# Top-32 attention and two MLPs on one core: PReLU with the threshold as bias, one reciprocal per pair, Mish in batches, and eight weight pieces split a round later

## The chip, the cores and the metric

The kernel runs on one core of one Trainium2 chip. Its time is the device time of one execution in microseconds (us); lower is better. The engines are PE (TensorE), DVE (VectorE), ACT (ScalarE), POOL (GpSimd) and SP, which here only issues DMAs.

## What is computed

Inputs are q, k, v of shape (2, 8, 576, 64) and four weight matrices in 64-bit floats. Cut to what matters:

```python
scores = scale * q @ k.T                                # 576 x 576 for each of 16 heads
kth = np.partition(scores, -32, axis=-1)[..., -32:-31]
scores = np.where(scores >= kth, scores, -1e9)          # 32 largest of each row stay
attn = np.exp(scores - max); attn = attn / (attn.sum() + 1e-9)
x = (attn @ v), heads side by side                      # 1152 tokens x 512
h = x @ w_in;  g = h * tanh(softplus(h));  x = g @ w_out     # MLP 1, Mish, d_ff = 2048
h = x @ w_in2; r = max(h, 0); out = (r * r) @ w_out2         # MLP 2, squared ReLU
```

## The kernel before

**Rounds, pairs, tiles.** The 1152 tokens go through in four rounds of 192, 320, 320 and 320. Attention for one round and two heads is a pair (20 pairs: 4, 4, 8, 4 by round, since round 2 takes 64 tokens of batch 0 and 256 of batch 1). A pair has one to five tiles of 128 rows, 72 in all: 12, 20, 20 and 20 by round. A tile (`tile_of`, L397) is: scores on PE (`ps`, L419), copied by ACT to `s`; the 32 largest of each row on DVE by four MAX8 and three MATCH_REPLACE8 (L435 to L439); two small POOL instructions that make biases from the 32nd value (L450, L451); a PReLU on ACT that pushes the smaller scores far down, then Exp with the row sum kept in `acc`; five PE transposes (L464, L466) and a copy to `pt`. `unit_end` (L486) inverts the sums of each unit of one or two tiles and spreads them (L492 to L499). `pair_end` (L503) multiplies by v (`px`, L519), transposes the inverses, and scales on DVE into `x` (L547).

**Weights.** The weights lie as 64-bit floats in 32 pieces of 1 MB. `convert` (L635 to L675) makes 32-bit floats: a PReLU on ACT, a TENSOR_SCALAR on POOL (L654), a SCALAR_TENSOR_TENSOR on DVE (L656, "combine" below). Round 0 multiplies by these in one float32 term. Meanwhile each piece is split into a high part (ACT, or POOL for every third) and a low part (four POOL subtractions of 256 columns, L294), and both parts are written back to DRAM. Rounds 1 to 3 fetch them (L700, 1 MB each) and use three fp32r products instead of one: `product`, L723.

**MLP.** Per round PE runs four phases of 64 output tiles by 128 rows: in (MLP 1), out, in (MLP 2), out. After the first, ACT applies Mish straight from PSUM and POOL subtracts for the low part `gl` (L283); after the third, ACT does ReLU, Square and the high part, POOL the low part. Mish and Exp lie in different ACT tables, so going from one to the other loads a table (ACT_TABLE_LOAD). Before a round, `x` is split into `xh` (ACT) and `xl` (DVE, L283).

**What sets the order.** The program is written by a small planner (`Order`, L82): each step is a generator that asks for an engine with a cost and a rank, and the instructions are emitted in the order in which the planner grants them. Each engine runs its own list strictly in that order, SP its list of DMA issues too. Buffers are counted by semaphores (`BUFS`): three `vt`, two `kr`, two `qr`, and seven 1 MB weight buffers (`ROLES`), which become the ring of fetched pieces when the conversion is done. `load(p)` takes kr, qr and vt together and starts when pair p-2 is prepared.

Of the kernel before, what the change touches and what calls it, by code (L numbers as in the profile page):

```python
# [18 lines left out]
UP = 2.0 ** 40  # L19
LOW3 = 2.0 ** -29 * (1.0 - 2.0 ** -12)  # L20
# [172 lines left out]
def topk_attention_two_mlps(  # L193
# [5 lines left out]
    v_rest: bass.AP,  # L199
# [106 lines left out]
    started, fast_done = Ev(), Ev()  # L306
    loaded, prepared = [Ev() for _ in pairs], [Ev() for _ in pairs]
# [6 lines left out]
    def load(p):  # L314
        b, s0, n = group(p)
        hp = pairs[p][2]
        h = slice(2 * hp, 2 * hp + 2)
        moves = []
        eng = nc.scalar if p == 0 else nc.sync
        halves = [slice(i * D, i * D + D) for i in range(2)]  # L320
        if owner[b, hp][0] == p:
            yield sems["kr"]
            kr = krs[p] = new([P, 2, S], F32, "kr")
            moves += [(kr[z], k[b, h].rearrange("h d s -> d h s"), 288) for z in halves]
        yield sems["qr"]
        qr = qrs[p] = new([P, 2, NMAX], F32, "qr")
        moves += [(qr[z, :, 0:n], q[b, h, :, s0:s0 + n].rearrange("h d s -> d h s"), n / 2) for z in halves]
        if p == 0:
            moves = [moves[i] for i in (0, 2, 1, 3)]
        yield sems["vt"]  # L330
        vt = vts[p] = new([P, 2, NK + 1, D], F32, "vt")
        last = [(vt[:, :, 0:NK, :], v[b, hp], 256), (vt[SR:P, :, NK, :], v_rest[b, hp], 32)]
        for i, (o, x, kb) in enumerate(moves):
            f = lambda o=o, x=x, e=eng if i % 2 else nc.sync: e.dma_start(out=o, in_=x)
            if i < len(moves) - 1:
                yield ("SP", 0.6, 5, f)
                sim.dma_free = max(sim.dma_free, sim.now + 0.8) + kb / 360.0
                if p == 0 and i == 1:
                    yield sim.dma_free - sim.now + 1.2
                    sim.set(started)  # L340
            else:
                yield from sim.dma(f, kb, 5)
        sim.set(loaded[p])
        for o, x, kb in last:
            yield ("SP", 0.6, 6, lambda o=o, x=x: nc.sync.dma_start(out=o, in_=x))
            sim.dma_free = max(sim.dma_free, sim.now + 0.8) + kb / 360.0

    def loads():
        for p in range(len(pairs)):
            if p > 1:  # L350
                yield prepared[p - 2]
# [45 lines left out]
    def tile_of(p, j, a, rank, unit, pair):  # L397
# [29 lines left out]
        yield act(0.65, 9, s.rearrange("p (a b) -> p a b", a=2), sp[:, :, 0:HK])  # L427
# [4 lines left out]
        nm = sb.tile([P, 2], F32, tag="nm", bufs=6, name="nm")  # L432
# [53 lines left out]
    def unit_end(j, unit, pair):  # L486

        acc, _, done = unit[:3]
        yield sems["r"]
        r_ = new([P, 2, D], F32, "r")  # L490
        z = acc if j < 2 else acc[:, 0:1]
        yield ("POOL", 0.35, 1, lambda: nc.gpsimd.tensor_scalar(out=z, in0=z, scalar1=1e-9, scalar2=None, op0=ALU.add))  # L492
        yield SLACK
        yield ("DVE", 0.16, 3, lambda: nc.vector.reciprocal(z, z))
        if j < 2:
            sums = acc[:, 0:2].rearrange("p (a o) -> p a o", o=1).to_broadcast([P, 2, D])
            yield ("POOL", 0.45, 1, lambda: nc.gpsimd.tensor_tensor(out=r_, in0=sums, in1=one2, op=ALU.mult))
        else:
            yield act(0.3, 10, r_, same, scale=z)  # L499
        pair["r"][j] = r_.rearrange("p a d -> p (a d)")  # L500
        sim.set(unit[5])

    def pair_end(p, units, pair):  # L503
# [3 lines left out]
        vt = vts[p]  # L507
        for u in units:
            for d in u[2]:
                yield d  # L510
        yield sems["ps_x"]
# [17 lines left out]
        for u in units:  # L529
            yield u[5]  # L530
        yield sems["ps_t"]
        pp = psum("t")

        def transposes():
            for t in range(nt):
                nc.tensor.matmul(pp[:, t * P:(t + 1) * P], pair["r"][t], ident, start=True, stop=True)
            if m:
                nc.tensor.matmul(pp[:, nt * P:n], pair["r"][2], sel, start=True, stop=True)

        yield ("PE", 0.25 * (nt + m), 7, transposes)  # L540
        for _ in range(nt + m):
            give("r")
        inv = sb.tile([P, NMAX], F32, tag="inv", bufs=1, name="inv")
# [7 lines left out]
        yield SLACK / 2
        yield ("DVE", 0.6, 4, scaled)
        give("ps_x")
        x1_left[r] -= 1
        if x1_left[r] == 0:
            sim.set(x1_done[r])

    def masks_done(j, unit, pair):
        for d in unit[1]:
            yield d  # L560
        yield from unit_end(j, unit, pair)

    x1_left = [HP * len(g) for g in ROUNDS]
# [68 lines left out]
    boths = Places(sim, [("w", i) for i in range(nw) if ROLES[i] == "b"], NP, to_ring)  # L632
    halves = Places(sim, [("half", i, h) for i in range(nw) if ROLES[i] == "w" for h in range(2)], NP - len(once), to_ring)

    def convert(i, raw_at):  # L635
# [26 lines left out]
        if HI[i % len(HI)] == "a":  # L662
# [271 lines left out]
```

## Time and profile before

| what | us |
|---|---|
| median of 3 runs | 714.75 |
| lowest, highest | 711.21, 715.51 |
| the profiled execution | 715.83 |
| its span, first to last instruction | 714.0 |

The span is what the trace shows; 1.8 us lie around it. All times of rows are counted from the span's start. PE is busy 608.3 us, DVE 447.2, ACT 435.6 and POOL 376.2. A busy time is a mean over stages with different limits, so the rows below are read stage by stage.

### The profile page before, as it was taken

To read this page: it belongs to the slowest core of one execution; us is meant where nothing else is said; L and a number is where in the kernel's file an instruction comes from. 1 tells how busy PE (TensorE), PEld (TensorE's weight loads), DVE (VectorE), ACT (ScalarE), POOL (GpSimd) and SP (SyncE) were. 2 spreads that over 40 slices of the span, in tenths; PEclk is the share of its full clock that TensorE was granted. 3 is DMA by queue.
4 is the path that set the end of the run, shared out by engine and by line. 5 is a ranking of instruction groups with operands and counts; after the bars stand their busy time and mean duration, and the time that the engine had idled before them with its cause. 6 is when DMAs were issued, how large, how long until landed. Compare 5 with 4: busy or idle time off the path is not lost.

```text
span 714.0 us, 11305 instructions
## 1 busy us (share of the span) xinstructions
PE 608.3 (85%) x4016; PEld 562.5 (79%) x4016; DVE 447.2 (63%) x841; ACT 435.6 (61%) x810; POOL 376.2 (53%) x584
## 2 busy tenths in 40 slices
PE   4344657789798778998889999989999999999997
PEld 2233447668796658898779999878899999999997
DVE  5978999888788884369788999999950000000000
ACT  3654767988488757854368955899745704512720
POOL 5998892489989997364455621334112401400410
PEclk9666779899999999999999999999999999999999
DMA  8786963377899899999966667643476888888850
GB/s 278 256 264 224 314 233 132 137 259 289 338 403 352 315 326 336 351 321 309 305 235 222 212 225 258 215 177 127 177 280 224 298 318 282 298 304 304 297 205 29
DMA packets 42362, 186.21 MB, mean 261 GB/s; under 512 B 8513, under 2 KB 19777, under 8 KB 21825
## 3 DMA queue, kind: packets, MB, share of 16 engines
q1 hardware_dynamic: 42016, 185.29, 74.1%
q8 instruction: 32, 0.52, 0.3%
q10 hardware_dynamic: 288, 0.20, 0.1%
q14 instruction: 26, 0.20, 0.1%
HBM read 149.55 MB, written 35.91 MB: 260 GB/s over the span
## 4 chain that ended last, share of the span: by engine, by line
PE 46%; POOL 26%; DMA 12%; ACT 7%; issue 4%; DVE 3%; SPq 0%; POOLq 0%; ACTq 0%; DVEq 0%
PE pm L723 39%; POOL w L294 10%; DMA qr<-in_q 5%; POOL stage L654 4%; DMA vt<-in_v 4%; DMA w<-both 3%; PE ps L419 2%; PE px L519 2%; ACT e L277 2%; ACT L277 2%; PE pt L464 2%; POOL w L287 2%; POOL w L654 2%; POOL kT L362 1%; POOL acc L492 1%
## 5 line engine op out<-in xcount | busy, mean ns | idle before, releaser
L723 PE MATMUL pm<-xh,w 128*128 128x320 f32 (+1 forms) x896 | 199.5, 315 | 3.9 <-DMA w<-both 1.8
L723 PE MATMUL pm<-gh,w 128*128 128x320 f32 x768 | 176.8, 312 | 0.0
L439 DVE MAX8 mx<-w 128x8 f32<-128x576 f32 x216 | 164.4, 761 | 7.4
L723 PEld LDWEIGHTS pm<-xh,w 128*128 128x128 f32 x896 | 152.3, 190 | 5.9 <-ACT h L277 2.2
L283 POOL TENSOR_TENSOR gl<-h,gh 128x320 fp32r<-128x320 f32 x96 | 83.5, 880 | 133.6 <-ACT gh L277 129.9
L723 PEld LDWEIGHTS pm<-gh,w 128*128 128x128 f32 x768 | 130.4, 189 | 0.4 <-issue 0.4
L723 PE MATMUL pm<-xl,w 128*128 128x320 f32 x384 | 119.7, 312 | 0.1
L723 PE MATMUL pm<-gl,w 128*128 128x320 f32 x384 | 119.1, 310 | 0.0
L438 DVE MATCH_REPLACE8 w<-mx,w 128x576 f32<-128x576 f32 x144 | 107.0, 743 | 0.0
L464 PE MATMUL pt<-ident,e 128*128 128x128 f32 x288 | 50.3, 303 | 56.0 <-ACT e L277 45.6
L277 ACT ACTIVATE e<-s,nm 128x576 f32<-128x576 f32 x72 | 55.5, 773 | 60.5 <-POOL nm L450 60.3
L294 POOL TENSOR_TENSOR w<-w,w 128x256 fp32r<-128x256 f32 x112 | 84.0, 779 | 9.1 <-ACT w L277 7.9
L464 PEld LDWEIGHTS pt<-ident,e 128*128 128x128 f32 x288 | 37.1, 153 | 64.4 <-ACT e L277 51.0
L723 PEld LDWEIGHTS pm<-xl,w 128*128 128x128 f32 x384 | 73.0, 190 | 0.3 <-DVE xl L283 0.3
L277 ACT ACTIVATE pt<-pt 128x640 f32<-128x640 f32 x72 | 50.8, 705 | 36.2 <-PE pt L466 35.8
L723 PEld LDWEIGHTS pm<-gl,w 128*128 128x128 f32 x384 | 72.6, 189 | 0.0
L277 ACT ACTIVATE h<-pm 128x320 f32<-128x320 f32 (+1 forms) x112 | 45.8, 422 | 37.9 <-PE pm L723 30.5
L435 DVE MAX8 mx<-s 128x8 f32<-128x576 f32 x72 | 53.7, 745 | 22.7 <-ACT s L277 22.7
L277 ACT ACTIVATE e<-e,nm 128x576 f32<-128x576 f32 x72 | 55.9, 776 | 6.0
L277 ACT ACTIVATE s<-ps 128x576 f32<-128x576 f32 x72 | 45.9, 637 | 12.7 <-PE ps L419 12.7
L438 DVE MATCH_REPLACE8 w<-mx,s 128x576 f32<-128x576 f32 x72 | 53.5, 743 | 0.0
L519 PE MATMUL px<-pt,vt 128*64 128x320 f32 (+7 forms) x400 | 50.6, 393 | 2.1 <-ACT pt L277 1.9
(101 smaller groups left out, 938.1 us busy)
## 6 DMA issues: line engine op xcount, KB each, us to landing
w<-both SPq DMA_DIRECT2D x96, 1024.0 KB, 5.0
both<-w SPq DMA_DIRECT2D x32, 1024.0 KB, 5.4
stage<-in_weights SPq DMA_DIRECT2D x22, 1024.0 KB, 6.1
w<-in_weights SPq DMA_DIRECT2D x10, 1024.0 KB, 5.9
vt<-in_v SPq DMA_DIRECT2D x20, 256.0 KB, 8.6
kr<-in_k SPq DMA_DIRECT2D x16, 288.0 KB, 12.6
qr<-in_q SPq DMA_DIRECT2D x16, 160.0 KB, 5.4
out_x<-y SPq DMA_DIRECT2D x8, 160.0 KB, 3.5
```

Of the source, the lines that this page charges most:

```text
L277: op = ("ACT", t, rank, lambda: nc.scalar.activation(out, in_, func, **kw))
L283: return ({"g": "POOL", "v": "DVE"}[e], t, rank, lambda: eng.tensor_tensor(out=out, in0=in0, in1=in1, op=ALU.subtract))
L287: return ("POOL", 0.08 + 0.00113 * n, rank, lambda: nc.gpsimd.tensor_copy(out=out, in_=in_))
L294: yield ("POOL", 0.05 + 0.0024 * n, rank, lambda: nc.gpsimd.tensor_tensor(out=out[:, z], in0=in0[:, z], in1=in1[:, z], op=op))
L419: nc.tensor.matmul(sp[:, i, 0:HK], q_, k_[:, i * HK:(i + 1) * HK], start=l == 0, stop=l == len(steps) - 1)
L435: nc.vector.max(out=mx[:, 0, :], in_=s)
L438: nc.vector.match_replace(out=w, in_to_replace=mx[:, i - 1, :], in_values=s if i == 1 else w, imm_value=LOWEST)
L439: nc.vector.max(out=mx[:, i, :], in_=w)
L464: nc.tensor.transpose(pp[:, c * P:(c + 1) * P], e[:, c * P:(c + 1) * P], ident)
L519: nc.tensor.matmul(xo[a * D:(a + 1) * D, 0:n], vt[z, a, c, :], pt[z, a, c, 0:n], start=c == 0, stop=c == NK)
L654: yield ("POOL", 1.3, 4, lambda: nc.gpsimd.tensor_scalar(out=lo, in0=lo.bitcast(U32), scalar1=LOW3, scalar2=-0.499, op0=ALU.mult, op1=ALU. ...
L723: nc.tensor.matmul(o, w[a], x[b], start=first and i == 0, stop=last and i == len(terms) - 1)
```

## The change

- **PReLU's bias is the threshold.** The copy of the scores multiplies by 2^40, PReLU computes threshold minus score with the 32nd value as bias, and Exp turns the sign back. One POOL instruction per tile goes (L450), and PReLU no longer waits for POOL; Exp still needs `nm`.
- **Sums inverted per pair.** One add on POOL and one reciprocal on DVE for all sums of a pair; PE spreads them by multiplying the broadcast sums with the identity (`spread`), beside the last tiles and not after px. `r`, `sel` and `same` go.
- **Mish in batches** (`BATCHES`: 4, 4, 4, 2, 2 tiles in rounds 0 to 2): ACT copies each tile to an SBUF buffer `hs` and runs Mish, then the high part, over a batch.
- **Squares** move from ACT to POOL in rounds 0 to 2 and to DVE in round 3 (`RELU`).
- **x split early**: each 128-row chunk of x is split when its pairs are done (`prepare_x`), not when all are.
- **Late pieces**: pieces 24 to 31 are not split in round 0 (`AHEAD`); they are kept as 512 KB of float32, fetched in round 1 into a second buffer, split there, and written back for rounds 2 and 3. All high parts are ACT's now (`HI`).
- **Loads**: v has its own process (`load_v`), so k and q no longer wait for a `vt` buffer. k, q and v are laid out on the host so that each is one DMA. `ROLES` has six buffers instead of seven; `hs` takes two of 4 x 320 columns.

```diff
-BUFS = {"s": 3, "e": 2, "r": 3, "w": 2, "kr": 2, "vt": 3, "qr": 2, "kT": 4, "h": 3, "x1": 2, "pt": 1, "y": 2}
+BUFS = {"s": 3, "e": 2, "w": 2, "kr": 2, "vt": 3, "qr": 2, "kT": 4, "h": 3, "hs": 2, "x1": 2, "pt": 1, "y": 2}
-HI = "aag"
-ROLES = "wwwbbbr"
+BATCHES = [[4, 4, 4, 2, 2]] * 3 + [[]]
+RELU = "pppv"
+XL = " vvv"
+HI = "a"
+AHEAD = 24
+ROLES = "wwwbbr"
...
+    def load_v():
+        for p in range(len(pairs)):
+            b = group(p)[0]
+            yield sems["vt"]
+            yield loaded[p]
+            vt = vts[p] = new([P, 2, NK + 1, D], F32, "vt")
+            yield from sim.dma(lambda: nc.sync.dma_start(out=vt, in_=v[b, pairs[p][2]]), 320, 6)
+            sim.set(v_loaded[p])
...
-        yield ("POOL", 0.7, 1, biases)
-
-        yield act(0.8, 8, e, s, AF.Prelu, "exp", bias=nm[:, 0:1], scale=UP, alpha=2.0 ** 120)
+        yield ("POOL", 0.38, 1, lambda: nc.gpsimd.tensor_scalar(out=nm, in0=thr, scalar1=mx[:, 0, 0:1], scalar2=scale / UP, op0=ALU.subtract, op1=ALU.mult))
+
+        yield act(0.8, 8, e, s, AF.Prelu, "exp", bias=thr, scale=-1.0, alpha=FALL)
         give("s")
-        yield act(0.85, 8, e, e, AF.Exp, "exp", bias=nm[:, 1:2], scale=scale / UP, accum_out=acc[:, a:a + 1])
+        yield act(0.98, 8, e, e, AF.Exp, "exp", bias=nm, scale=-scale / UP / FALL, accum_out=acc[:, a:a + 1])
...
+        def spread():
             for t in range(nt):
...
+                for a in range(2):
+                    nc.tensor.matmul(pp[a * D:(a + 1) * D, t * P:(t + 1) * P], acc[:, t, a:a + 1].to_broadcast([P, D]), ident, start=True, stop=True)
...
+        if i >= AHEAD:
+            kept[i] = dr.tile([P, n], F32, tag=f"k{i}", name=f"kept{i}")
+            sim.spawn(put_back(i, w_at))
+            yield from sim.dma(lambda: nc.sync.dma_start(out=kept[i], in_=w), 512, 15)
+            sim.set(kept_done[i])
+            return
...
+    def fetch_late(i, j, at, w_at):
+        rings[i] = at
+        both = shared[at].rearrange("p (a m) -> p a m", a=2)
+        ready[i] = [both[:, 0], both[:, 1]]
+        w = shared[w_at][:, 0:NW].bitcast(F32)
+        yield from sim.dma(lambda: nc.sync.dma_start(out=w, in_=kept[j]), 512, 12)
+        yield from split_w(j, both, w, HI1[j % len(HI1)], 7)
+        ring.append(w_at)
+        sim.give(ring_sem)
+        sim.set(got[i])
+        yield from store(j, both)
...
+        def batch(i0, m_, hs):
...
+                yield act(t, 2, hs[:, 0:m_, 0:n], hs[:, 0:m_, 0:n], AF.Mish, "mish")
+                yield act(t, 11, g[0][:, z, 0:n], hs[:, 0:m_, 0:n])
+                for i in range(0, m_, 2):
...
+                    yield sub("g", 2 * n, 5, g[1][:, u, 0:n], hs[:, y, 0:n], g[0][:, u, 0:n].bitcast(F32))
...
+            if RELU[r] == "p":
+                yield ("POOL", 0.1 + 0.0024 * n, 5, lambda: nc.gpsimd.tensor_tensor(out=h_out, in0=h, in1=h, op=ALU.mult))
+            elif RELU[r] == "v":
+                yield ("DVE", 0.2 + 0.001 * n, 3, lambda: nc.vector.tensor_tensor(out=h_out, in0=h, in1=h, op=ALU.mult))
```

Three places in the engines' lists follow. On DVE, where round 1's last x (`x_1141`, after the change `x_1189`) is scaled and split; `x_2212` and `x_2178` belong to round 2. Before:

```order
L439 MAX mx<-w 128x8
L547 TENSOR_TENSOR x_1141<-px,inv 128x320
L656 SCALAR_TENSOR_TENSOR w_93<-w_93,stage 128x1024
L438 MATCH_REPLACE w<-mx,w 128x576
L439 MAX mx<-w 128x8
L494 RECIPROCAL acc<-acc 128x1
L283 TENSOR_TENSOR xl<-x_1141,xh 128x320 x2
L547 TENSOR_TENSOR x_2212<-px,inv 128x64
L283 TENSOR_TENSOR xl<-x_1141,xh 128x320 x2
L435 MAX mx<-s 128x8
```

The same place after the change:

```order
L431 MAX mx<-w 128x8
L527 RECIPROCAL acc<-acc 128x1
L512 TENSOR_TENSOR x_1189<-px,inv 128x320
L427 MAX mx<-s 128x8
L430 MATCH_REPLACE w<-mx,s 128x576
L431 MAX mx<-w 128x8
L512 TENSOR_TENSOR x_2178<-px,inv 128x64
L430 MATCH_REPLACE w<-mx,w 128x576
L431 MAX mx<-w 128x8
L276 TENSOR_TENSOR xl<-x_1189,xh 128x320
```

All 32 combines and three of the four splits now stand ahead of the last x, which comes after tile 34 as before; only one split is left behind it.

On SP, the loads of k and q for the first pair of batch 1 (the first 576-column k of round 2) and the fetches of round 1 (`w<-both`) around them. Before:

```order
L345 DMA vt<-in_v_rest 64x2x64
L334 DMA kr<-in_k 64x2x576 x2
L334 DMA qr<-in_q 64x2x256 x2
L700 DMA w_2148<-both_704 128x2048
L700 DMA w_95<-both_789 128x2048
L700 DMA w_2216<-both_817 128x2048
L700 DMA w_96<-both_834 128x2048
L700 DMA w_2346<-both_1149 128x2048
L700 DMA w_2092<-both_1157 128x2048
L345 DMA vt<-in_v 128x2x256
L345 DMA vt<-in_v_rest 64x2x64
L334 DMA kr<-in_k 64x2x576 x2
```

After, from the first such load on:

```order
L321 DMA kr<-in_k 128x1152
L321 DMA qr<-in_q 128x2x256
L702 DMA w_1928<-both_367 128x2048
L645 DMA kept_1929<-w_85 128x1024
L645 DMA kept_1957<-w_86 128x1024
L961 DMA out_x<-y 128x192
L702 DMA w_1990<-both_370 128x2048
L702 DMA w_2002<-both_476 128x2048
L665 DMA both_2001<-w_88 128x2048
L702 DMA w_87<-both_518 128x2048
L645 DMA kept_2034<-w_86 128x1024
L321 DMA kr<-in_k 128x1152
```

The first of these loads now stands ahead of every fetch of round 1, the second behind four; before they stood behind six and twelve.

On POOL, in round 1's third phase (ReLU of MLP 2). Before:

```order
L283 TENSOR_TENSOR gl<-h,gh 128x320 x2
L450 TENSOR_SCALAR nm<-mx 128x1
L451 TENSOR_SCALAR nm<-mx 128x1
L492 TENSOR_SCALAR acc<-acc 128x2
L283 TENSOR_TENSOR gl<-h,gh 128x320 x2
```

After:

```order
L936 TENSOR_TENSOR h<-h 128x320 x2
L276 TENSOR_TENSOR gl<-h,gh 128x320
L441 TENSOR_SCALAR nm<-mx 128x1
L276 TENSOR_TENSOR gl<-h,gh 128x320
L287 TENSOR_TENSOR w_1928<-w_1990,w_1928 128x256 x3
L936 TENSOR_TENSOR h<-h 128x320
L276 TENSOR_TENSOR gl<-h,gh 128x320
```

The squares (L936) and the low parts of the first late piece (`w_1928<-w_1990`) stand between the subtractions that the next phase needs.

## Rows read from the trace of the kernel before

**Rows 1.** The page: busy tenths in 40 slices of 17.85 us

```profile
PE   4344657789798778998889999989999999999997
...
DVE  5978999888788884369788999999950000000000
...
POOL 5998892489989997364455621334112401400410
```

**Rows 2.** Stretches: us, then busy us (x count) by engine, granted clock, DMA share, GB/s

```profile
226.00:275.00 49.00, 36.21 (x254) 30.75 (x252) 38.48 (x69) 32.05 (x56) 45.26 (x64) 1.00 0.90 314
275.00:313.00 38.00, 35.45 (x268) 33.99 (x268) 15.10 (x33) 27.25 (x54) 23.46 (x32) 1.00 1.02 372
...
597.00:714.00 117.00, 113.08 (x768) 112.58 (x768) 3.54 (x8) 42.26 (x92) 28.07 (x32) 1.00 0.68 241
```

**Rows 3.** Groups by line, DVE, 8 to 265 us: busy, mean ns, idle before

```profile
L656 DVE SCALAR_TENSOR_TENSOR w<-w,stage 128x1024 int32<-128x1024 int32 x19 | 24.0, 1261 | 17.7 <-POOL stage L654 13.4 <-ACT w L277 4.2
L656 DVE SCALAR_TENSOR_TENSOR w<-w,w 128x1024 int32<-128x1024 int32 x9 | 11.5, 1275 | 6.5 <-POOL w L654 6.5
```

**Rows 4.** Timeline, DVE and PE, end of round 1's attention: start, us, instruction, idle

```profile
118.47 0.74 DVE L435 MAX8 mx<-s 128x8 f32<-128x576 f32 x1
...
124.08 0.74 DVE L435 MAX8 mx<-s 128x8 f32<-128x576 f32 x1
...
265.34 0.76 DVE L439 MAX8 mx<-w 128x8 f32<-128x576 f32 x1
...
271.44 0.99 DVE L283 TENSOR_TENSOR xl<-x,xh 128x320 fp32r<-128x320 f32 x2 [5.27 <-ACT xh L277]
...
274.81 0.41 PE L723 MATMUL pm<-xh,w 128*128 128x320 f32 x1
```

**Rows 5.** Groups by line, POOL, 113 to 275 us

```profile
L294 POOL TENSOR_TENSOR w<-w,w 128x256 fp32r<-128x256 f32 x84 | 64.3, 794 | 6.7 <-ACT w L277 5.6
...
L287 POOL CAST w<-w 128x1024 fp32r<-128x1024 f32 x7 | 10.4, 1488 | 0.3
...
L450 POOL TENSOR_SCALAR nm<-mx 128x1 f32<-128x1 f32 x20 | 6.5, 323 | 7.3 <-DVE mx L439 5.9
```

**Rows 6.** Timeline, ACT, one change from Mish to Exp in round 0

```profile
123.38 0.33 ACT L277 ACTIVATE first<-pm 128x192 f32<-128x192 f32 x1 [0.62 <-PE pm L723]
123.73 1.28 ACT L277 ACT_TABLE_LOAD   x1
125.03 0.78 ACT L277 ACTIVATE e<-s,nm 128x576 f32<-128x576 f32 x1
```

**Rows 7.** Timeline, SP's issues and the DVE tile that waited for them

```profile
281.86 1.46 SPq L334 DMA_DIRECT2D kr<-in_k  x2
285.22 4.30 SPq L334 DMA_DIRECT2D qr<-in_q  x2
291.42 8.65 SPq L700 DMA_DIRECT2D w<-both  x6
...
309.23 0.76 DVE L435 MAX8 mx<-s 128x8 f32<-128x576 f32 x1 [7.39 <-ACT s L277]
```

**Rows 8.** Waits of PE, 275 to 541 us: us in total, times, longest

```profile
PE pt L536 <- POOL r L497: 3.4, 1, 3.4
PE ps L419 <- POOL kT L362: 2.7, 2, 2.0
PE pt L464 <- ACT e L277: 2.6, 1, 2.6
```

**Rows 9.** Groups by line, whole run: high parts on ACT, transposes of inverses on PE

```profile
L277 ACT ACTIVATE w<-w 128x1024 fp32r<-128x1024 f32 (+1 forms) x28 | 30.4, 1086 | 2.3 <-DMA both<-w 1.7 <-DVE w L656 0.6
...
L536 PE MATMUL pt<-ident,r 128*128 128x128 f32 x56 | 10.0, 292 | 4.6 <-POOL r L497 3.4 <-ACT pt L277 1.2
```

**Rows 10.** Groups by line, POOL, 540 to 597 us, when DVE is idle

```profile
L283 POOL TENSOR_TENSOR gl<-h,gh 128x320 fp32r<-128x320 f32 x16 | 14.1, 879 | 25.6 <-ACT gh L277 24.7 <-PE pm L723 0.9
```

**Rows 11.** The page: DMA issues, KB each, us to landing

```profile
w<-both SPq DMA_DIRECT2D x96, 1024.0 KB, 5.0
```

More of the change, by code (lines that the diff above doesn't have):

```diff
@@ L484, in tile_of @@
         sim.set(done[a])
[L486 to L501, printed above, removed]
     def pair_end(p, units, pair):
@@ L506, in pair_end @@
         nt, m = tiles(n)
-        vt = vts[p]
+        for u in units:
+            for d in u[1]:
+                yield d
+        z = pair["acc"].rearrange("p u a -> p (u a)")[:, 0:2 * nt + m]
+        yield ("POOL", 0.33, 1, lambda: nc.gpsimd.tensor_scalar(out=z, in0=z, scalar1=1e-9, scalar2=None, op0=ALU.add))
+        sim.spawn(inverse(p, pair, z))
         for u in units:
@@ L510, in pair_end @@
                 yield d
+        yield v_loaded[p]
+        vt = vts[p]
         yield sems["ps_x"]
@@ L528, in pair_end @@
                 yield 0.5
[L529 to L543, printed above, removed]
+        yield pair["inv_done"]
+        inv = pair["inv"]
         o = sum(x[2] for x in ROUNDS[r][:gi])
@@ L547, in scaled, with inverse @@
             nc.vector.tensor_tensor(out=x1[r][:, hp, o:o + n], in0=xo[:, 0:n], in1=inv[:, 0:n], op=ALU.mult)
+        yield ("DVE", 0.25 + 0.0009 * n, 4, scaled)
+        give("ps_x")
+        x1_left[r][hp] -= 1
+        if x1_left[r][hp] == 0:
+            sim.set(x1_part[r][hp])
+        if not any(x1_left[r]):
+            sim.set(x1_done[r])
+    def inverse(p, pair, z):
+        n = group(p)[2]
+        nt, m = tiles(n)
+        acc = pair["acc"]
+        yield SLACK / 2
+        yield ("DVE", 0.16, 3, lambda: nc.vector.reciprocal(z, z))
+        yield sems["ps_t"]
+        pp = psum("t")
+        def spread():
+            for t in range(nt):
+                for a in range(2):
+                    nc.tensor.matmul(pp[a * D:(a + 1) * D, t * P:(t + 1) * P], acc[:, t, a:a + 1].to_broadcast([P, D]), ident, start=True, stop=True)
+            for a in range(2 * m):
+                h = slice(a * D, (a + 1) * D)
+                nc.tensor.matmul(pp[h, nt * P:n], acc[h, nt, 0:1].to_broadcast([D, D]), ident[h, h], start=True, stop=True)
+        yield ("PE", 0.25 * nt + 0.15 * m, 7, spread)
+        inv = pair["inv"] = sb.tile([P, NMAX], F32, tag="inv", bufs=1, name="inv")
         yield act(evict_time(n), 9, inv[:, 0:n], pp[:, 0:n])
         give("ps_t")
[L551 to L563, printed above, removed]
+        sim.set(pair["inv_done"])
+    x1_left = [[len(g)] * HP for g in ROUNDS]
+    x1_part = [[Ev() for _ in range(HP)] for _ in ROUNDS]
     def attention():
@@ L712, in release, with late @@
     def release(i):
+        def late():
+            yield both_done[i % NP]
+            ring.append(rings.pop(i))
+            sim.give(ring_sem)
         if i < NP:
@@ L715, in release @@
         else:
-            ring.append(rings.pop(i))
-            sim.give(ring_sem)
+            sim.spawn(late())
     def product(o, w, x, first, last):
@@ L892, in all_mlps @@
             yield from mlps(r)
-    for process in (loads(), preparations(), attention(), conversions(), fetches(), all_mlps()):
+    for process in (loads(), load_v(), preparations(), attention(), conversions(), fetches(), all_mlps()):
         sim.spawn(process)
```

217 lines of the change are left out of this document (128 added, 89 removed).

## The prediction

> **What bounds the kernel now.** I read the slices first [rows 1]. There the reader sees two halves. Up to about slice 16 (285 us) DVE and POOL stand at 8 or 9 tenths while PE stands at 4 to 8; from slice 21 on PE stands at 9 almost throughout, and in the last ten slices DVE has nothing to do. So the end is set by PE's work from the moment that it is fed, and that moment, the start of round 1, is set by DVE and POOL. The stretches [rows 2] put numbers to it: between 226 and 275 us POOL is busy 45.26 of 49 us (92%) and PE 36.21; in round 3, 597 to 714 us, PE is busy 113.08 us for 768 matmuls, 0.147 us each, at the full granted clock. A microsecond by which round 1 starts earlier is then a microsecond at the end, as long as PE is not starved later.
>
> Next, what holds up DVE before round 1. Back to back, a tile takes 124.08 - 118.47 = 5.61 us [rows 4]. Up to the end of tile 34, whose last MAX8 ends at 265.34 + 0.76 = 266.1 us [rows 4], DVE's list holds 34 tiles (191 us) and 32 combines of 1.26 us (40 us) [rows 3]: 231 us, plus the start-up and waits. The waits stand on the combines: 17.7 + 6.5 = 24.2 us, nearly 20 of them for POOL's TENSOR_SCALAR on the same piece [rows 3]. POOL is late because it is full: the low parts of pieces cost 84 x 794 ns in 113 to 275 us, the high parts that POOL makes 1488 ns each [rows 5].
>
> Last, the seam. Round 1's first matmul runs at 274.81, 8.7 us after tile 34's end; 5.27 of them are DVE's wait for `xh` before it can make `xl` [rows 4].
>
> **The change part by part.** The sum is made against the profiled execution, 715.8 us (span 714.0 and 1.8 around it), 1.1 above the median.
>
> *POOL before round 1.* By the lists, the stretch of tiles 13 to 32 loses 20 of 79 low-part instructions (20 x 0.794 = 15.9 us), six high parts (6 x 1.488 = 8.9) and one of two `nm` instructions in 20 tiles (20 x 0.323 = 6.5) [rows 5]; it gains 16 squares of 192 columns, by columns 0.879 x 192 / 320 = 0.53 us each [rows 10], 8.4 us. Net 23 us less on an engine that was 92% busy at the end of that stretch [rows 2], so the TENSOR_SCALAR that a combine waits for stands in a shorter queue. DVE's own work stays: same tiles, same combines. Of the 24.2 us, zero to all can go; I take 20, since four fifths of them are waits for POOL: **-20**.
>
> *The seam.* Three of four `xl` now stand ahead of the last x, and one behind it, two DVE steps into tile 35. The 5.27 us wait goes, and a single xh and xl remain; against that, PE's list has the scores and transposes up to tile 38 ahead of the rest of round 1. Bounds 0 and -6: **-4**.
>
> *First load.* k comes as one DMA of 576 KB, where PE began on a first half of 288. At 314 GB/s [rows 2] the rest is 0.9 us; bounds 0 and 2: **+1**, since DVE's chain hangs on the first scores.
>
> *Nothing on the path:* reciprocals (44 to 20) are DVE crumbs. Mish in batches adds a copy per tile and takes away table loads; where it shows is round 0, where ACT goes Mish to Exp and back [rows 6], six loads of 1.28 us, against 16 copies of 0.33: 7.7 against 5.3. The cover is ACT's idle time, 32.05 of 49 us busy in 226 to 275 us [rows 2]; without it 5 us. Here a rule can be weighed. The trace has the load begin as the instruction before it ends and the next one begin 0.02 us after the load [rows 6]: a switch costs 1.28 us. The Trainium skill, ScalarE: Activation LUTs, section What ACT_TABLE_LOAD costs, has a drain of 1.38 us on top, 2.66 in all. By it the six loads would give 8 us more, and the forecast would be 685; no such drain stands in these rows.
>
> *From round 1 to the end* took 714.0 - 274.8 = 439.2 us. PE's waits there for `r` (3.4), for `kT` (2.7) and for `e` (2.6) [rows 8] are what the change aims at: `r` is gone, PReLU waits no more for POOL, and k and q are issued ahead of the fetches. Zero to 8.7 can go; I take **-8**. The DVE stall behind those loads is much longer: k and q were issued at 281.9 and 285.2, six fetches followed, and DVE's next tile started at 309.23 [rows 7]; DVE was busy 15.10 of 38 us in 275 to 313 [rows 2]. But PE was busy 35.45 of these 38 with round 1, so its removal alone is worth 2.5 us at most and is in the -8. It matters as cover: after the change PE has less MLP work ahead of the last px (1312 matmuls of all 2560 against 1402, counted in the lists), so DVE has less room to be late.
>
> *New PE work.* The spread takes two matmuls where the transpose took one. The old ones are busy 10.0 us in 56 records [rows 9], doubled 10 more, of which 16 of 28 fall after round 1's start: up to 5.7, less where they overlap: **+4**.
>
> *POOL in the third phase.* Per output tile PE needs 12 x 0.147 = 1.76 us, POOL now a square and a subtraction, 2 x 0.879 = 1.76 [rows 10]. In round 2 they tie. In round 1 POOL's list has 14 low parts of late pieces and 8 `nm` among them: 28.2 + 14 x 0.794 + 8 x 0.323 = 42 us, against 28 for the matmuls and the attention that PE has in between. Bounds 0 and 14; I take **+3**, near the lower end, since PE has eight tiles to do there. A rule speaks against this move. The same subtraction costs 0.879 / 320 = 2.75 ns a column with DVE idle [rows 10], and 794 / 256 = 3.10 in round 0, where DVE combines [rows 5], 13% more. The Trainium skill, Perfetto Trace Analysis, section Optimizing Scalar/DVE Operations, says that the two share a read port, so that moving work between them might not help. By it, 13% on 42 us would add 5.5 us, and the forecast would be 698.
>
> *Late pieces.* Eight pieces of 0.5 MB are fetched, split and written back in round 1's last phase. I take **+1**: they are fetched ahead, and the split needs 4 x 0.794 us of POOL [rows 5] and 1.1 of ACT [rows 9], engines with time to spare; the upper bound is the rival below. Round 3's squares go from ACT to DVE, both idle there (3.54 of 117 us) [rows 2]: 0.
>
> Sum: -20 - 4 + 1 - 8 + 4 + 3 + 1 = -23; 715.8 - 23 = 692.8, so I forecast **693**.
>
> **Rivals.**
>
> *The waits do not go (713).* Each combine still passes ACT, POOL and DVE in lists of fixed order, and POOL's freed time goes to whatever is next. For it: part of rows 3 is a wait for ACT (4.2), and DVE's list is as tight as before. Against: POOL's load falls by 23 us just there. Price: the -20 stays out, 693 + 20 = 713, within 1%.
>
> *Everything hidden (677).* All 24.2 go, the seam gives 6, the waits 8.7, and spread, POOL and late pieces cost nothing: 715.8 - 38.9 = 677. For it: DVE's stall after 275 us goes too, so attention runs ahead. Against: POOL's list in the third phase.
>
> *Late pieces in single file (734), on the other side.* A late piece needs two of six ring buffers. If only one is under way at a time, each costs a fetch (between half of the 5.0 of 1 MB and all of it [rows 11], take 4.3), ACT's 1.1 [rows 9] and POOL's 4 x 0.79 = 3.2: 8.6 us, while PE eats a piece in 24 x 0.147 = 3.5. That is 5.1 x 8 = 41 us of PE idle, 693 + 41 = 734. It decides from the point where pieces come more than 3.5 us apart. ACT and POOL would also stand still in their lists behind each fetch, with `nm` and Exp behind them. Against: the fetches stand ahead of the phase, and with two under way the excess is 0.8 x 8 = 6.
>
> **How the numbers follow.** Forecast 0.50, all hidden 0.22, waits stay 0.17, single file 0.11. A difference of 1% is about what a measurement of this kernel can tell from no change. The forecast and the hidden case lie below that bound (0.72), and a third of the case in which waits stay, which is not sharp, does too: faster 0.78. The rest of that case is within 1%, with a little of the single file: 0.13. Slower 0.09. The likeliest case's own range is 683 to 703; the range that holds 8 in 10 leaves out most of the single file and the tail of the hidden case: 670 to 714.
>
> **What would show it.** Right: DVE's idle time ahead of the combines falls from 24 us to about 4; round 1's first full group of matmuls begins near 252 us; k and q of round 2 come before the fetches and DVE loses no 20 us after round 1's start; from there on PE takes about 439 us as before. Wrong: the combines wait as before (waits stay); PE waits for `gl` or for a weight buffer in round 1's last two phases for more than 5 us, with the SP list standing on a kept piece (single file); or PE idles for `e` in round 1 because attention, not PE, has become the bound.

## The result and the profile after

The changed kernel takes 683.55 us (median of 4 runs, 682.52 to 686.53) where the kernel before took 712.98 on the same chip: ratio 0.9601, 95% interval 0.9537 to 0.9666. The forecast was 693, the range 670 to 714. The profiled execution's span is 682.8 us, 31.2 less than before. Line numbers below are the changed kernel's: matmuls L741, top-k L427, L430, L431, combines L638, low parts L287, squares L936.

The page, busy times and the slices that answer to [rows 1]; a slice is 17.07 us:

```profile
PE 608.7 (89%) x4104; PEld 559.7 (82%) x4104; DVE 464.1 (68%) x832; ACT 406.0 (59%) x723; POOL 356.2 (52%) x478
...
PE   4456569998969799979999999999999999999998
...
DVE  5979999999888999988999999997500100001410
...
POOL 7998662597996565760238886023207703501420
```

PE has the same busy time (608.3 before), so the whole gain is PE's idle time. In slices 13 to 15, the last ahead of round 1, POOL stands at 6, 5 and 6 tenths where it stood at 9, and DVE has lost its dip of slices 17 and 18. Three stretches that answer to [rows 2] (engines in the order PE, PEld, DVE, ACT, POOL):

```profile
205.00:251.40 46.40, 40.30 (x258) 33.92 (x257) 42.72 (x74) 27.24 (x45) 30.65 (x42) 0.96 0.96 375
251.40:296.00 44.60, 41.55 (x346) 38.69 (x344) 39.76 (x82) 36.73 (x64) 26.99 (x30) 1.00 0.97 385
567.40:682.80 115.40, 111.97 (x770) 111.71 (x768) 15.58 (x20) 33.13 (x74) 28.28 (x32) 1.00 0.72 256
```

In the first, POOL is busy 66% of the time (92% before). In the second, at round 1's start, DVE is busy 39.76 of 44.6 us where it was 15.10 of 38. The third is round 3, with the squares on DVE. It is 1.7 us shorter: PE idles 0.5 us less, and its 768 matmuls take 1.2 us less at the same clock. No run shows why.

DVE's waits from 8 to 266 us, which answer to [rows 3], in all, times, longest:

```profile
DVE w L638 <- POOL w L636: 3.5, 2, 2.5
DVE w L638 <- issue: 2.4, 1, 2.4
DVE w L638 <- POOL stage L636: 1.5, 3, 0.7
...
DVE xl L638 <- POOL stage L636: 1.0, 1, 1.0
DVE stage L638 <- POOL w L636: 1.0, 1, 1.0
```

Combines wait 9.4 us. [rows 3] has 24.2 us for 28 of the 32 combines; the other four waited 2.1 us more, so like for like 26.2 us fell to 9.4. The other four before:

```profile
DVE stage L656 <- POOL w L654: 1.0, 1, 1.0
DVE xl L656 <- POOL stage L654: 0.9, 1, 0.9
DVE first L656 <- POOL stage L654: 0.2, 1, 0.2
```

The seam, DVE and PE, which answers to [rows 4]:

```profile
253.58 0.76 DVE L431 MAX8 mx<-w 128x8 f32<-128x576 f32 x1
...
258.68 0.47 DVE L276 TENSOR_TENSOR xl<-x,xh 128x320 fp32r<-128x320 f32 x1
...
259.64 0.41 PE L741 MATMUL pm<-xh,w 128*128 128x320 f32 x1
```

Tile 34 ends at 254.3 us (266.1 before). Nine matmuls of round 1 had run at 251.4; the body goes on at 259.64, after the last `xl`.

To compare kernels I cut each span at two matmuls: the 20th of round 1 (the body begins) and the first of round 3. With them stand the end of the last combine and of tile 34, all us from the span's start, read from the traces:

| kernel | ratio (95%) | last combine | tile 34 | body | rounds 1, 2 | rest |
|---|---|---|---|---|---|---|
| before | 1 | 264.6 | 266.1 | 277.9 | 319.0 | 117.1 |
| after | 0.9601 (0.9537 to 0.9666) | 243.1 | 254.3 | 261.2 | 306.2 | 115.4 |
| order redrawn | 0.9604 (0.9549 to 0.9659) | 244.0 | 255.2 | 262.1 | 308.3 | 115.3 |
| no late pieces | 0.9821 (0.9771 to 0.9871) | 267.6 | 251.3 | 278.1 | 307.5 | 115.3 |
| four late | 0.9796 (0.9731 to 0.9860) | 251.7 | 264.2 | 270.1 | 311.6 | 115.1 |
| twelve late | 0.9634 (0.9591 to 0.9677) | 239.6 | 252.5 | 259.4 | 312.6 | 115.1 |
| no batches | 0.9805 (0.9732 to 0.9878) | 254.8 | 259.5 | 266.8 | 312.4 | 117.1 |
| a third of high parts on POOL | 0.9741 (0.9697 to 0.9784) | 248.1 | 256.9 | 264.3 | 314.1 | 115.4 |
| x split late | 0.9661 (0.9615 to 0.9707) | 244.9 | 254.2 | 259.3 | 310.1 | 117.1 |
| v with k | 0.9678 (0.9628 to 0.9729) | 246.7 | 259.4 | 262.2 | 309.8 | 117.1 |
| squares on ACT | 0.9658 (0.9590 to 0.9726) | 240.1 | 254.6 | 262.3 | 308.2 | 115.3 |
| before + late | 1.0220 (1.0135 to 1.0305) | 267.3 | 262.4 | 280.1 | 330.8 | 116.7 |
| before + batches | 0.9998 (0.9969 to 1.0028) | 259.6 | 261.1 | 273.4 | 320.2 | 116.7 |
| before + both | 1.0104 (1.0060 to 1.0148) | 252.8 | 264.1 | 277.4 | 324.0 | 116.7 |

The gain of 31.2 us is 16.7 up to the body, 12.8 in rounds 1 and 2, and 1.7 after. Up to the body PE's idle time fell by 22.3 us (86.6 to 64.3) and its busy time grew by 5.6, with 60 more matmuls outside the MLP. Rounds 1 and 2 in the kernel before, in the changed kernel, and with a third of the high parts on POOL (columns as above):

```profile
277.93:596.89 318.96, 303.77 (x2121) 286.33 (x2119) 212.11 (x421) 203.49 (x403) 119.78 (x217) 0.98 0.75 255
261.21:567.42 306.21, 299.82 (x2149) 280.37 (x2148) 213.10 (x406) 194.47 (x355) 138.49 (x190) 0.99 0.72 262
264.34:578.49 314.15, 305.59 (x2148) 284.03 (x2148) 212.62 (x405) 196.97 (x357) 138.68 (x190) 0.97 0.70 256
```

There PE's idle time fell from 15.2 to 6.4 us and its busy time by 4.0.

### The profile page after: what moved, and what is told of

Read it like the earlier page. It is cut to its first block, busy times and chain, and to the rows that moved or that the text cites. A ratio compares the mean times of both kernels' runs of the same rounds, so it can differ in the third digit from the quotient of the medians.

```text
span 682.8 us, 11207 instructions
## 1 busy us (share of the span) xinstructions
PE 608.7 (89%) x4104; PEld 559.7 (82%) x4104; DVE 464.1 (68%) x832; ACT 406.0 (59%) x723; POOL 356.2 (52%) x478
## 4 chain that ended last, share of the span: by engine, by line
PE 58%; DVE 22%; POOL 11%; ACT 3%; issue 3%; DMA 3%; DVEq 0%; POOLq 0%; ACTq 0%
PE pm L741 48%; DVE w L430 8%; DVE mx L431 7%; POOL w L287 4%; DVE w L638 4%; PE ps L411 3%; PE px L497 3%; DVE mx L427 2%; PE pt L452 2%; POOL stage L636 2%; POOL gl L276 1%; DMA stage<-in_weights 1%; ACT w L270 1%; POOL nm L441 1%; DMA w<-kept 1%
## 5 line engine op out<-in xcount | busy, mean ns | idle before, releaser
L741 PE MATMUL pm<-xh,w 128*128 128x320 f32 (+1 forms) x896 | 200.2, 315 | 5.5 <-ACT xh L270 2.8
L741 PE MATMUL pm<-gh,w 128*128 128x320 f32 x768 | 177.8, 313 | 0.0
L431 DVE MAX8 mx<-w 128x8 f32<-128x576 f32 x216 | 164.4, 761 | 7.4
L741 PEld LDWEIGHTS pm<-xh,w 128*128 128x128 f32 x896 | 152.7, 191 | 7.2 <-ACT xh L270 3.1
L741 PEld LDWEIGHTS pm<-gh,w 128*128 128x128 f32 x768 | 131.0, 189 | 0.7 <-issue 0.3
L741 PE MATMUL pm<-gl,w 128*128 128x320 f32 x384 | 119.7, 312 | 2.2 <-POOL gl L276 2.2
L741 PE MATMUL pm<-xl,w 128*128 128x320 f32 x384 | 119.1, 310 | 0.0
L430 DVE MATCH_REPLACE8 w<-mx,w 128x576 f32<-128x576 f32 x144 | 106.9, 742 | 0.0
L276 POOL TENSOR_TENSOR gl<-h,gh 128x320 fp32r<-128x320 f32 x64 | 56.2, 884 | 85.0 <-ACT gh L270 84.0
L287 POOL TENSOR_TENSOR w<-w,w 128x256 fp32r<-128x256 f32 x112 | 82.8, 763 | 23.3 <-ACT w L270 19.0
L441 POOL TENSOR_SCALAR nm<-mx 128x1 f32<-128x1 f32 x72 | 31.8, 441 | 85.4 <-DVE mx L431 74.1
L741 PEld LDWEIGHTS pm<-gl,w 128*128 128x128 f32 x384 | 72.8, 190 | 3.0 <-POOL gl L276 2.9
L741 PEld LDWEIGHTS pm<-xl,w 128*128 128x128 f32 x384 | 72.2, 188 | 0.0
L276 DVE TENSOR_TENSOR xl<-pm,xh 128x320 fp32r<-128x320 f32 x12 | 5.9, 488 | 96.8 <-ACT xh L270 96.7
L270 ACT ACTIVATE e<-e,nm 128x576 f32<-128x576 f32 x72 | 55.7, 773 | 19.3 <-POOL nm L441 15.2
L427 DVE MAX8 mx<-s 128x8 f32<-128x576 f32 x72 | 53.5, 743 | 15.9 <-ACT s L270 15.9
L270 ACT ACTIVATE e<-s,mx 128x576 f32<-128x576 f32 x72 | 55.0, 770 | 15.4 <-DVE mx L431 15.2
L430 DVE MATCH_REPLACE8 w<-mx,s 128x576 f32<-128x576 f32 x72 | 53.5, 743 | 0.0
```

What stands on the lines that cost most here:

```text
L270: op = ("ACT", t, rank, lambda: nc.scalar.activation(out, in_, func, **kw))
L276: return ({"g": "POOL", "v": "DVE"}[e], t, rank, lambda: eng.tensor_tensor(out=out, in0=in0, in1=in1, op=ALU.subtract))
L287: yield ("POOL", 0.1 + 0.0026 * n, rank, lambda: nc.gpsimd.tensor_tensor(out=out[:, z], in0=in0[:, z], in1=in1[:, z], op=op))
L427: nc.vector.max(out=mx[:, 0, :], in_=s)
L430: nc.vector.match_replace(out=w, in_to_replace=mx[:, i - 1, :], in_values=s if i == 1 else w, imm_value=LOWEST)
L431: nc.vector.max(out=mx[:, i, :], in_=w)
```

## The experiments

**Order redrawn.** `CONV_EVERY = 2.8` to `2.9`: the planner's order changes and no work does.

> The changed kernel with one planner constant moved: conversions are offered every 2.9 us instead of 2.8. No work is added or taken away; only the order of the lists is drawn anew. If the gain comes from the work that was moved, the time stays at 683.6 within 4 us. If it comes from a lucky order, it moves by 8 us or more.

0.9604, as the changed kernel: the gain does not hang on this one order, though one redraw cannot exclude luck. Body and rounds 1 and 2 shift by 0.9 and 2.1 us, so differences of that size in one stretch prove nothing. The run with high parts on POOL, below, shifts rounds 1 and 2 by 7.9 us though it changes no work there.

**Late pieces, none, four, twelve.** `AHEAD = 24` to 32, 28 and 20.

> The changed kernel with all 32 pieces split in round 0 (AHEAD = 32), no late pieces. Theory (POOL's load before round 1 sets DVE's waits for combines): POOL gets 8 x 4 x 0.76 = 24 us back ahead of or around round 1's start, DVE's idle time up to tile 34 grows from 18 us to about 28, round 1 starts some 8 us later, and round 1 saves at most the 2 us that PE waits for gl: 689 to 693 us. Rival (the late pieces cost in round 1 what they save in round 0): 680 to 686.

> The changed kernel with four late pieces (28 to 31) in place of eight. With none it took 15.8 us longer than with eight. Theory (each early split at the end of round 0 holds the buffer that a later combine waits for, one after the other): about half of that, last combine 252 to 258 us, 691 to 697 us. Rival (it is a threshold; four suffice to free the buffers): 684 to 688 us. Other rival (what costs is the traffic of stores beside round 1's fetches, not the combines): last combine below 248 us and the loss in round 1's body.

> The changed kernel with twelve late pieces in place of eight. Theory (with eight the combines no longer end last: round 1's body waits for the attention tiles ahead of it, and twelve late splits load POOL in round 1's third phase): last combine at 243 us or before, 685 to 692 us, no gain. Rival (the splits still hold the combines): 679 to 683 us, a version that beats both kernels.

Without late pieces the kernel needs 15.7 us more ((0.9821 - 0.9601) x 714), and both numbers that I had put down are too low. All of it lies before the body. DVE's waits for combines do not come back (4.3 + 2.9 + 1.1 + 1.0 = 9.3 us), and tile 34 ends at 251.3, earlier than in the changed kernel. What is late is the last combine. ACT's and DVE's timelines without late pieces, then with four:

```profile
263.97 1.13 ACT L270 ACTIVATE w<-stage 128x1024 f32<-128x1024 f32 x1 [2.57 <-POOL w L287]
...
266.38 1.21 DVE L638 SCALAR_TENSOR_TENSOR w<-w,stage 128x1024 int32<-128x1024 int32 x1
```

```profile
249.31 1.12 ACT L270 ACTIVATE w<-stage 128x1024 f32<-128x1024 f32 x1 [6.27 <-DMA kept<-w]
...
250.52 1.23 DVE L638 SCALAR_TENSOR_TENSOR w<-w,stage 128x1024 int32<-128x1024 int32 x1 [4.61 <-ACT w L270]
```

Without late pieces the piece's first step, ACT's write into a half of a weight buffer, waits for POOL's low part of an earlier piece: that piece keeps its half until it has been split. With eight late pieces the same combine runs at 241.88.

With four, the theory does not hold. The last combine ends at 251.7, a third of the way, but the time is 698 us, within 2 us of that without late pieces. The body begins 8.9 us later because tile 34 ends 9.9 us later (264.2 against 254.3). What the rows above show is the copy of a late piece to DRAM (`kept`, issued at 236.64 us): until it lands, it holds the half that the next piece needs, and tile 34 stands behind that piece's combine in DVE's list. That is 4.6 of the 9.9 us; the rest I did not follow. So a late piece gives its half back by its copy, where an early one does by its split. The changed kernel has such a wait of ACT too (6.28 us ahead of 212.05), and 2.4 of the 9.4 us of its combines follow it. Another 5.4 us are lost in rounds 1 and 2.

With twelve, the combine ends at 239.6 but tile 34 still at 252.5, the body gains 1.8, and rounds 1 and 2 lose 6.4: no gain, as expected. That the late splits cost PE time in the third phase is not shown: it waits for no `gl` there, but in rounds 1 and 2 6.3 us for `e` (2.5 in the changed kernel).

**Mish without batches.** `BATCHES = [[]] * 4`.

> The changed kernel with Mish group by group from PSUM as in the kernel before (no hs, no batches). Theory (the table loads lie beside work of PE, whose stream is the bound): 0 to 3 us longer, 684 to 689 us by this job's comparison, with some ten more table loads on ACT. Rival (the loads stand in the way of the exponentials on ACT, for which PE's transposes wait): 8 to 12 us longer, 692 to 696 us, with PE's waits for e and pt longer by that.

The rival is nearer, and its band too low: (0.9805 - 0.9601) x 714 = 14.6 us. By the traces 5.6 us lie before the body, 6.2 in rounds 1 and 2 and 1.7 in round 3. In 103 to 160 us ACT's loads are, first without batches, then in the changed kernel:

```profile
L270 ACT ACT_TABLE_LOAD x10 | 12.8, 1283 | 0.2
```

```profile
L270 ACT ACT_TABLE_LOAD x4 | 5.1, 1283 | 0.1
L270 ACT ACTIVATE hs<-pm 128x192 f32<-128x192 f32 x16 | 4.9, 322 | 2.8 <-PE pm L741 2.7
```

With batches a PSUM tile is free after a copy of 322 ns that needs no table, so PE goes through round 0's first phase in 22 us (103.8 to 125.7); without, it takes until 147.3. There PE had finished three tiles by 125.5 us, and their Mish stood at 136.01, behind 9 us of conversions, exponentials and copies and a table load; the phase's next matmuls ran at 142.01:

```profile
136.01 0.78 ACT L270 ACTIVATE first<-pm 128x192 f32<-128x192 f32 x3
...
142.01 2.22 PE L741 MATMUL pm<-x,w 128*128 128x192 f32 x12
```

So what holds the tiles is the place of Mish in ACT's list, where the planner ranks a change of table low (`STAY`), more than the 1.28 us of a load. A stretch of the run without batches, then of the changed kernel (columns as above):

```profile
127.00:153.00 26.00, 22.71 (x129) 18.50 (x130) 24.83 (x43) 22.82 (x37) 14.50 (x21) 0.80 0.59 218
```

```profile
127.00:153.00 26.00, 26.00 (x176) 23.55 (x175) 25.45 (x39) 22.18 (x34) 22.98 (x28) 1.00 0.78 296
```

PE makes 129 matmuls instead of 176, stands idle 3.3 us, and its mean granted clock is 0.80. The pieces come free later, and the last combine ends at 254.8. PE's waits for `e` ahead of the body are 12.6 us against 3.3, as the rival has it, but 7.7 of them end at 222.5 and 240.6 us, and ACT loads no table from 160 to 262 us.

**High parts.** `HI = "a"` to `"aag"`.

> The changed kernel with every third high part on POOL again (as in the kernel before) in place of ACT. Theory of the prediction (POOL's load before round 1 is what DVE's combines wait for; some 6 us of its 20 came by the high parts): 4 to 8 us longer, 690 to 694 us by this job's comparison, DVE's waits for combines up from 9 us. Rival (POOL now has room, the chains are those of use and splits): within 2 us of the changed kernel, 684 to 688 us.

The time is the theory's, the mechanism is not shown. The run's waits of combines, 5 to 256 us:

```profile
DVE w L638 <- POOL w L636: 3.4, 3, 2.5
DVE w L638 <- POOL stage L636: 3.3, 6, 1.0
DVE stage L638 <- POOL w L636: 1.1, 1, 1.1
DVE xl L638 <- POOL stage L636: 1.0, 1, 1.0
```

That is 8.8 us, not more than the 9.4, though POOL is busy 40.6 us in 205 to 256 us against 31.0. The body is 3.1 us late, and 7.9 us go in rounds 1 and 2, where this constant changes only the order. By the rows above PE's idle time grows there by only 2.2 us; the other 5.8 are busy time of the same matmuls at a mean granted clock of 0.97 against 0.99.

**x split late.** The split of x moves back to the start of its round.

```diff
+        yield x1_done[r]
+        sim.spawn(prepare_x(r))
...
-        if r + 1 < NR:
-            sim.spawn(prepare_x(r + 1))
```

> The changed kernel with x split only when the MLP of its round begins, after all of x is done, as before the change. Theory (the seams between rounds are part of the gain): xh and xl stand between two rounds again; before the change PE's gap there was 5.6 us ahead of round 1, 4.4 ahead of round 2 and 0.9 ahead of round 3, of which round 1's stays filled in part by tiles: 5 to 9 us, 689 to 692. Rival (PE has attention work to do there, so the split is hidden): 682 to 686.

(0.9661 - 0.9601) x 714 = 4.3 us, just under the theory's 5 to 9, with a median of 690.2 us in its band; the intervals overlap. The place is plain: between rounds 1 and 2 PE's MLP stands still from 433.8 to 438.2 us, and by 0.9 between rounds 2 and 3.

**v with k.** The `vt` buffer is awaited in `load`, ahead of k and q, as before.

```diff
+        yield sems["vt"]
+        vts[p] = new([P, 2, NK + 1, D], F32, "vt")
```

> The changed kernel with v's buffer taken in load() again, so that k and q of a pair wait for a free vt buffer; v's DMA itself stays after q. Theory (the loads of k and q were behind the DVE stall after round 1's start, and PE's waits in round 1 hang on it): DVE loses some 20 us between tiles 35 and 41 again, PE's loss in round 1 grows by 5 to 10 us: 688 to 694. Rival (PE has enough of round 1 to do, the stall is hidden): 682 to 686.

(0.9678 - 0.9601) x 714 = 5.5 us, in the theory's band, but the intervals overlap. DVE's waits from 251 to 340 us with v beside k, then in the changed kernel:

```profile
DVE mx L428 <- ACT s L270: 14.5, 2, 9.1
```

```profile
DVE mx L427 <- ACT s L270: 3.5, 2, 3.0
```

DVE's stall is back, but its price is not shown: PE's idle time in rounds 1 and 2 is 6.5 us as in the changed kernel (6.4), which is what the rival says of that stretch. PE idles 3.4 us more ahead of the body; the rest is busy time, 1.7 us of it in round 3, where no attention is left.

**Squares on ACT.** `RELU = "pppv"` to `"aaaa"`.

> The changed kernel with rounds 1 to 3's squares of gelu's groups on ACT in all rounds (none on POOL or DVE). Theory (POOL's square in front of gl costs PE 2.2 us in round 1 and up to 3 us in all; ACT has the room): 0 to 3 us shorter, 681 to 686 us. Rival (ACT is the busier neighbour: the squares stand ahead of exponentials): 4 to 8 us longer, 688 to 692 us.

Inconclusive: 4.1 us longer by the ratios, inside both intervals. It is not faster, and the 2.2 us could not be had this way. PE waits for `gl` at 306.11 and 307.92 us of the changed kernel, in round 1's second phase, where `gl` are the low parts of Mish, not of the squares:

```profile
304.50 1.55 POOL L276 TENSOR_TENSOR gl<-hs,gh 128x640 fp32r<-128x640 f32 x1
```

```profile
306.11 0.41 PE L741 MATMUL pm<-gl,w 128*128 128x320 f32 x1 [1.52 <-POOL gl L276]
```

With the squares on ACT 1.9 us of this wait stay, and PE's waits for `e` grow from 2.5 to 6.0 us. (The squares are those of MLP 2's ReLU; the expectation's "gelu" is a slip.)

**The parts alone.** The kernel before with late pieces, with batches (for the room one weight buffer less), and with both.

> The kernel before with the late pieces alone: pieces 24 to 31 are kept whole in round 0 and split in round 1, nothing else of the change is made. Theory (the splits hold the buffers of the last weight pieces, so that the last combine ends at 265 us in the kernel before and at 266 us in the changed kernel with 32 early splits, against 243 us with 24): last combine near 245 us, round 1's matmuls 14 to 17 us earlier, 697 to 702 us. Rival (the late pieces pay only beside the other edits, since POOL keeps its work on sums, nm and -U*threshold): 708 to 714 us, last combine after 258 us.

> The kernel before with Mish in batches from SBUF alone (for the room: one weight buffer less, as in the changed kernel, one output buffer less, five mx in place of six). Theory (the weight pieces leave round 0 by two chains that end together: PE's use of a piece, which Mish in PSUM holds up in round 0's first phase, and the splits, which hold its buffer; one alone frees nothing): round 0's first phase takes some 22 us in place of 42, but the last combine still ends at 255 us or later, and the time is 704 to 716 us. Rival (the batches carry the gain by themselves): last combine before 250 us, 698 to 703 us.

> The kernel before with both: Mish in batches from SBUF and the late pieces (the room as in the run with batches alone). Theory of the two chains: last combine at 243 to 250 us, round 1 begins 12 to 18 us earlier than in the kernel before, 694 to 704 us, though each alone gives nothing. Rival (POOL's relief by sums, nm and squares is needed as well, or round 1 gives the gain back as with late pieces alone): 708 us or more.

Late pieces alone are 2.2% slower, batches alone, with their smaller buffers, change nothing, both together are 1.0% slower. Of my theories only that of the batches held, and there the first phase took 30 us where I had 22; for both together the rival's "708 us or more" came. Late pieces alone leave the last combine at 267.3, which would fit use and splits ending together. With both it ends at 252.8, yet tile 34 still at 264.1: DVE's idle time before it is 29.8 us against 32.1 before and 17.7 in the changed kernel (tile 34's end less the first MAX8's start less busy time). And rounds 1 and 2 lose. The chain of waits in "before + late", then in "before + both":

```profile
289.95 9.10 DMA kr<-in_k
...
299.70 8.44 DMA qr<-in_q
```

```profile
282.05 6.28 DMA qr<-in_q
...
311.14 7.53 DMA qr<-in_q
```

k and q land late behind `vt` and the fetches, as in [rows 7]. In the changed kernel SP issues them so:

```profile
263.45 0.43 SPq L321 DMA_DIRECT2D kr<-in_k  x1
263.94 0.55 SPq L321 DMA_DIRECT2D qr<-in_q  x1
264.53 0.60 SPq L337 DMA_DIRECT2D vt<-in_v  x1
266.76 8.55 SPq L702 DMA_DIRECT2D w<-both  x3
```

The loads stand ahead of vt and of the fetches that wait for buffers. That v apart would turn "before + both" into a gain was not tried.

## Why the prediction was right and where it was wrong

The direction and the range held, the forecast was 9 us too high. The sum put all of its 23 us on the way to round 1's body and the seam, with about nothing after; 16.7 came there, and 14.5 after. That the two errors, 6 us too much and 14.5 too little, partly cancel is luck.

*POOL before round 1, -20.* Right as a place, too large, and, as far as is known, given to the wrong instructions. The waits of all combines fell by 16.8 us (26.2 to 9.4; the groups of [rows 3] from 24.2 to 7.5, where I had said to about 4). DVE's idle time ahead of tile 34 fell by 14.4 us, its busy time grew by 3.0, and tile 34 ends 11.8 us earlier. But without late pieces, with the 20 low parts back and POOL busy 43.2 us in 205 to 256 us (31.0 in the changed kernel), those waits stay at 9.3, and with the high parts back at 8.8. So neither, undone alone, brings the waits back. The low parts matter through the halves of weight buffers, a chain that I did not price. Which of the other edits freed DVE (one `nm` per tile, sums per pair, the new cost of POOL's wide instructions in the planner) was not tried apart, and why the waits fell stays open. The lists' counts fit; POOL's groups, 113 to 275 us, which answer to [rows 5]:

```profile
L287 POOL TENSOR_TENSOR w<-w,w 128x256 fp32r<-128x256 f32 x56 | 42.6, 783 | 11.8 <-ACT w L270 11.3
...
L441 POOL TENSOR_SCALAR nm<-mx 128x1 f32<-128x1 f32 x22 | 12.8, 581 | 18.5 <-DVE mx L431 14.0 <-DVE acc L527 3.0
...
L936 POOL TENSOR_TENSOR first<-h 128x192 f32<-128x192 f32 x16 | 7.9, 503 | 2.2 <-ACT h L270 2.1
```

28 low parts fewer, and the squares cost 7.9 for 8.4 reckoned; but the `nm` that is left takes 581 ns, not 323 (the last section says why).

*The seam, -4.* From tile 34's end to the body 11.8 us became 6.9: -4.9. *First load, +1*: DVE's first MAX8 starts at 8.0 against 8.3: nothing.

*Nothing on the path: Mish in batches.* This step failed. I weighed 7.7 us of table loads against 5.3 of copies on an ACT with time to spare; what counts is that each Mish held a PSUM tile until its turn and its table came. Undoing it costs 14.6 us. The Trainium skill's drain (ScalarE: Activation LUTs, section What ACT_TABLE_LOAD costs) is no explanation: ACT stood idle 0.2 us ahead of ten loads, and the loads last 1283 ns.

*From round 1 to the end, -8 and +4 and +3 and +1.* This is the step with the wrong size: about 0, measured -14.5. PE's waits that answer to [rows 8], 251 to 520 us:

```profile
PE pt L452 <- ACT e L270: 2.5, 3, 1.2
PE pm L741 <- POOL gl L276: 2.2, 2, 1.5
PE pt L537 <- DVE acc L527: 1.1, 2, 0.6
```

The waits for `r` and `kT` are gone and that for `e` is the same, so 6 of the -8 came. POOL in the third phase costs nothing, where I took 3: the 2.2 us for `gl` lie in the second phase and come with the batches (the experiment with squares on ACT has the rows), and a square takes 722 ns, not 879. The late pieces cost nothing here either: PE waits for no weight buffer, and rounds 1 and 2 take 306.2 us with eight and 307.5 with none. Round 3's squares cost nothing either, though ACT was not idle there as I had it (42.26 of 117 us [rows 2]; 3.54 is DVE's). The spread was mis-sized. After the body's start its 88 matmuls take 6.4 us from start to start, none of it waiting (both waits for `acc` above lie ahead of the body); the 44 before took 10.2, 3.4 waiting. So 6.4 against 6.8 where I had added 4. In all, PE's idle time in rounds 1 and 2 fell by 8.8 us and its busy time by 4.0. Some 3 us of the busy time, by an estimate from the mean granted clocks of 0.98 and 0.99 over some 310 us, are the clock. Which edit brought the 8.8 is not settled. Undoing the early split of x (rounds 1 and 2: +3.9), v apart (+3.6) and the batches (+6.2) each lengthens this stretch, but so does a mere change of order (+7.9 with high parts on POOL), and with v beside k PE's idle time is no longer. Of the 1.7 us of round 3, 1.2 are no waits: the matmuls of its in phases follow each other at 144.4 ns on average, at 146.7 before, and at 148.8 with v beside k and without batches, all at the full granted clock. Why is open.

*The rivals.* "The waits do not go" fell with the waits. "Late pieces in single file" did not happen. "Everything hidden", 677, is 6.5 us off, nearer than the forecast, but not by its terms: 9.4 us of the combines' waits stayed.

The effects don't add: undoing late pieces, batches, v apart and the early split costs 15.7 + 14.6 + 5.5 + 4.3 = 40 us, more than the whole gain of 28.5 by the same ratios, and late pieces and batches put into the kernel before give nothing or less. Round 1's body waits for the last combine, for tile 34 and for PE's own round 0, which in the kernel before end within 5 us of each other (264.6, 266.1, 269.2).

## What to carry to other kernels

Where several chains end together at one point, price each edit by undoing it in the finished kernel, not by adding it to the old one: late pieces save 16 us in the finished kernel and cost 16 us in the old one. Copying a PSUM tile out at once let PE go on here, where a Mish that waited for its turn and its table stopped it, though ACT had time for both. For each buffer that a stream passes through, ask which step gives it back: here it was the split or, for a late piece, the copy to DRAM, and not the use alone.

## What the runs showed of the hardware

Combines on DVE and instructions on POOL shut each other out. Two places of the changed kernel's timeline:

```profile
156.07 1.22 DVE L638 SCALAR_TENSOR_TENSOR w<-w,w 128x1024 int32<-128x1024 int32 x1
156.13 1.32 POOL L441 TENSOR_SCALAR nm<-mx 128x1 f32<-128x1 f32 x1
```

```profile
130.71 2.38 POOL L636 TENSOR_SCALAR stage<-stage 128x1024 int32<-128x1024 uint32 x2
...
132.32 1.85 DVE L638 SCALAR_TENSOR_TENSOR w<-w,w 128x1024 int32<-128x1024 int32 x1
```

An `nm` takes 0.30 us (the median); the one above starts 0.06 after a combine, lasts 1.32 and ends 0.16 after it. Eight of 72 last 1.19 to 1.34 like it, and a ninth stands behind two combines for 2.2 us. A combine of 1.22 that starts with 0.77 of a POOL instruction left lasts 1.85; ten of 32 are over 1.4 us. The ten lose 4.6 us over 1.22 each (three such in the kernel before: 1.1), and the long `nm` make the mean of 581 ns. The Trainium skill, SBUF — State Buffer, section SBUF: two separate sides, has this rule: a DVE instruction with two SBUF inputs and a GpSimd one that reads SBUF hold the shared port in turn, each for its whole length. The trace agrees. MAX8 and MATCH_REPLACE8 slow POOL hardly at all. POOL's groups for `gl` and for the late low parts in round 1's third phase, 340 to 395 us, where no combine runs and each of the 13 `gl` lies beside a MAX8 or MATCH_REPLACE8:

```profile
L276 POOL TENSOR_TENSOR gl<-h,gh 128x320 fp32r<-128x320 f32 x13 | 11.4, 885 | 0.3 <-ACT gh L270 0.2
L287 POOL TENSOR_TENSOR w<-w,w 128x256 fp32r<-128x256 f32 x11 | 8.1, 761 | 1.2 <-ACT w L270 1.2
```

With DVE idle `gl` took 879 ns [rows 10], so the 13% that I had set against this phase did not come. Most of that 13% was the width: 256 columns take 2.97 ns a column here too, without a combine, against 3.10 in [rows 5] and 2.75 for 320 columns.
